# A second place for the high halves of keys and queries of three pairs, made earlier, and other float32 shares

## The chip, the cores and the metric

One core of a Trainium2 chip runs the whole program. The metric is the time of one execution on the device in microseconds (us), less is better. The core's engines are PE (TensorE: matmuls and the loading of their weights), DVE (VectorE), ACT (ScalarE), POOL (GpSimd) and SP (SyncE, which here only issues DMAs). Each engine takes its instructions in the order of its own list and waits at an instruction until what it needs is there.

## The reference

Three layers follow each other. Attention has 4 batches, 8 heads, 1152 positions and a head size of 64; neighbouring queries are averaged in twos (576 queries). A gated layer works on 2304 tokens of 512 numbers, and a soft mixture of 8 experts with 4 slots each comes last.

```python
q_pool = q.reshape(B, H, S // factor, factor, D).mean(axis=3)
scores = scale * np.matmul(q_pool, k.transpose(0, 1, 3, 2))
scores = scores - np.max(scores, axis=-1, keepdims=True)
attn = np.exp(scores)
attn = attn / (np.sum(attn, axis=-1, keepdims=True) + 1e-09)
return np.matmul(attn, v)

g = x @ w_gate
x = (g * (1.0 / (1.0 + np.exp(-g))) * (x @ w_val)) @ w_out

d = softmax of (x @ phi) over tokens;  slot_input = d.T @ x
slot_out[e] = np.maximum(slot_input[e] @ w1[e], 0.0) @ w2[e]
return (softmax of (x @ phi) over slots) @ slot_out
```

## The kernel before

Attention goes in 16 steps, one for each pair of heads; pairs and steps are counted from 0 here, so the "pairs 3, 5, 7" of the change's name are the pairs 2, 4 and 6. Every number is carried as a high and a low half in 16 bits.

**A step.** A step has 21 units. A unit's scores come from two matmuls into one bank (`unit`, L506 and L509). The second one adds the low halves and takes off the row's maximum, which lies in row D of the tile `QH`. ACT takes the exponential (L514), POOL makes the low half `PL` of the weights P (L523), and three units later the weights meet the values: three 16-bit matmuls per quarter (L550, L554, L555; L542 for the remainders), or, for a share of the units, one float32 matmul (L548), which needs no `PL`. The table `F32_PART` says how large that share is in each of the steps 0 to 7; in all others it is none.

**The maxima of the next pair.** While step i runs, `row_max` finds the row maxima of pair i + 1: 18 matmuls of 512 columns and 9 of 128 (L423) from the key's high half `kh` and from `QD`, which holds the two heads' queries on its diagonal and zeros beside it; each result is reduced by DVE (L429, L440). They share two banks (`mx`), so a matmul waits for the reduction two before it. When all are done, DVE makes `nm` (L443), ACT makes `mt` (L409) and issues the DMA (L449) that puts it into `QH`; the first L509 of step i + 1 waits for that DMA.

**The high halves.** `split_high` makes them: DVE adds the two neighbours of the queries in `qr` (L277), ACT casts `kh` and `qh` (L234), and DVE copies `qh` to `QD` in two pieces (L296). There is one tile each for `kh`, `qh` and `QD`, and the copies to `QD` are ordered behind the previous pair's `nm`. `split_pair` then makes the low halves `ql` (DVE, L325) and `kl` (POOL, L327) and moves everything to the places where the scores want it, by DMAs on SP's queue (L331 to L340).

**Other work.** From step 2 to step 8 the weights of the gated layer are prepared (L712 to L776), in step with the units; they go to six places `wgv`, the place `wgv[4]` in step 6. The gated layer itself (L811 to L816) takes part from step 4, again in step with the units, and runs on after attention; the experts come at the end. A scheduler puts the instructions in order for each engine when the program is built; `after` adds an order that it keeps.

The lines that the change and the steps below speak of:

```python
after(ins, (nm_name or nm_first)[-1])            # L297: QD behind the last nm
if steps[k - 1] in has_max and steps[k] in raw and steps[k] not in highs:   # L1168
    split_high(*steps[k])
```

Of the kernel before, what the change touches and what calls it, by code (L numbers as in the profile page):

```python
# [10 lines left out]
F16 = mybir.dt.float16  # L11
# [41 lines left out]
MOE_PACE = [(4, 0.0), (8, 1.0), (16, 5.8)]  # L53
PREP_BEG, PREP_END = 2, 8
FETCH_LEAD, FETCH_BEG = 2, 0.3
F32_PART = [0.17, 0.0, 0.17, 0.25, 0.33, 0.33, 0.34, 0.34]
F32_LAST = [99, 99, 99, 99, 99, 99, 11, 11]
VR_W = (2, 5)
VRB = 2
HNB = 1  # L60
SUBS = ["al", "l"]
# [23 lines left out]
def tile_pool_attention_glu_softmoe(  # L85
# [115 lines left out]
    nc.gpsimd.memset(KLs[1][D:D + 1, :, :], 16.0)  # L201

    QD = at.tile([P, 2, SQ], F16, name="QD")
    nc.gpsimd.memset(QD[:D, 1, :], 0.0)
    nc.gpsimd.memset(QD[D:, 0, :], 0.0)
    KHs = {}

    def load_pair(b, p):

# [61 lines left out]
    def split_high(b, p, first=None):  # L271

        kr, qr, _ = raw[b, p]

        r = slice(D if first else 0, P)
        qp = qr[r, 0, :]
        add = sub("a", b, p).tensor_tensor(out=qp, in0=qp, in1=qr[r, 1, :], op=ALU.add)  # L277

        if first:
            after(q_first[0], add.ins.name)  # L280
        if (b, p) == steps[1]:
            after(add, last_max[0])
        elif (b, p) == steps[2]:
            after(add, nm_name[-1])
        elif not first:
            not_before(add, ADD_LEAD)
        kh = at.tile([P, S], F16, tag="kh", bufs=1, name=f"kh{b}_{p}")
        KHs[b, p] = kh
        k_cast = cast("k", b, p, kh[r], kr[r])
        if mt_name:  # L290
            after(k_cast, mt_name[-1])
        qh = at.tile([P, SQ], F16, tag="qh", bufs=1, name=f"qh{b}_{p}")
        q_cast = cast("q", b, p, qh[r], qp).ins.name
        rows = [slice(0, D), slice(D, P)]
        for hd in range(0 if first else 2):
            ins = nc.vector.tensor_copy(out=QD[rows[hd], hd, :], in_=qh[rows[hd], :])  # L296
            after(ins, (nm_name or nm_first)[-1])  # L297
        highs[b, p] = r, qp, kh, qh, q_cast
        if first:
            highs_first.extend((kh, qh))  # L300
# [108 lines left out]
        return nc.scalar.activation(dst, src, AF.Copy, scale=-1.0 / 16.0, bias=math.log(PSC))  # L409

    NGQ = SQ // D
    mt_name, nm_name = [], []
    has_max = {steps[0]}

    def row_max(b, p):

        kh = KHs.pop((b, p))
        mp = at.tile([P, NGQ, 3], F32, tag="mp", bufs=2, name=f"mp{b}_{p}")
        R = S - 2 * QT

        def scores(t, g, k0, kw):
            q = QD.rearrange("p h q -> p (h q)")[:, g::NGQ]
            nc.tensor.matmul(t, q, kh[:, k0:k0 + kw], start=True, stop=True)  # L423

        for g in range(NGQ):
            for c in range(2):
                t = ps("mx", [P, QT], bufs=MXB, name=f"mx{b}_{p}_{g}_{c}")
                scores(t, g, c * QT, QT)
                ins = nc.vector.reduce_max(out=mp[:, g, c:c + 1], in_=t, axis=AX.X)  # L429
                if (b, p) == steps[1]:  # L430
                    mp_first.append(ins.ins.name)
                yield
            if g % 4 == 3 or g == NGQ - 1:

                g0 = g // 4 * 4
                n = g + 1 - g0
                t = ps("mx", [P, 4, R], bufs=MXB, name=f"mx{b}_{p}_{g}_r")
                for x in range(n):
                    scores(t[:, x, :], g0 + x, 2 * QT, R)
                nc.vector.reduce_max(out=mp[:, g0:g + 1, 2:3], in_=t[:, :n, :], axis=AX.X)  # L440
                yield
# [708 lines left out]
    for i, (b, p) in enumerate(steps):  # L1150
        for u, _ in enumerate(attn(b, p)):
# [13 lines left out]
                maxima(11 + int((MX0 - 11) * min(1.0, f / MX0_END)) + int(MXP * min(1.0, max(0.0, f - MX1_BEG) / (MX1_END - MX1_BEG))))  # L1165
            for k in (i + 1, i + 2):
                if 2 <= k < len(steps):
                    if steps[k - 1] in has_max and steps[k] in raw and steps[k] not in highs:  # L1168
                        split_high(*steps[k])
                    if steps[k] in highs or steps[k] in QHs:  # L1170
                        part = (i + f - (k - 1) - MX_BEG) / (MX_END - MX_BEG)
# [310 lines left out]
```

## Time and profile before

| what | value |
|---|---|
| median of 3 runs | 807.19 us |
| lowest and highest | 804.07 and 810.06 us |
| the profiled execution | 806.76 us |
| its span | 805.0 us |
| PE busy | 768.6 us (95%) |
| DVE, POOL and ACT busy | 521.2, 418.1 and 398.3 us |

The span is the time from the first to the last instruction; 1.8 us lie around it. A matmul's duration in the profile holds its way through the array, so a busy PE may still be able to take more: what one costs in a row of them is read from the distance between starts. An engine's idle time counts only where another one waits for it.

### The profile page before, as it was taken

How to read it: one execution, taken by the hardware profiler on the slowest of the kernel's cores; microseconds unless marked ns; L12 is line 12 of the kernel's file. 1: busy time of each engine (PE TensorE's matmuls, PEld its weight loads, DVE VectorE, ACT ScalarE, POOL GpSimd, SP SyncE). 2: the span in 40 equal slices, each digit the busy share in tenths (PEclk: the TensorE clock that was granted, in tenths of full speed). 3: DMA queues.
4: the chain of work that ended last, by engine and by line, in shares of the span. 5: the costliest groups of instructions: out<-in, count | busy, mean ns of one | idle time of the engine just before them, and what ended most of it. 6: DMA issues, size and time to landing. Idle time of an engine off the chain costs nothing.

```text
span 805.0 us, 23021 instructions
## 1 busy us (share of the span) xinstructions
PE 768.6 (95%) x9618; PEld 587.1 (73%) x9618; DVE 521.2 (65%) x1048; ACT 398.3 (49%) x770; POOL 418.1 (52%) x393
## 2 busy tenths in 40 slices
PE   6969889999999999999999999999999999999896
PEld 1546567687878777877787878777788988887544
DVE  6677889778687877676758675766552455455323
ACT  4545878777687844443544544444444222122112
POOL 9868876656567765755666666656555100000200
PEclk9989999999999999999999999999999999999799
DMA  8526878959777672533455455415112499269798
GB/s 246 140 78 194 224 199 252 236 178 210 201 230 190 200 155 61 130 94 89 116 146 138 100 117 143 90 28 107 28 27 42 99 318 279 54 184 224 255 419 359
DMA packets 115656, 132.42 MB, mean 165 GB/s; under 512 B 82272, under 2 KB 88352, under 8 KB 111328
## 3 DMA queue, kind: packets, MB, share of 16 engines
q1 hardware_dynamic: 113392, 130.92, 59.3%
q8 instruction: 75, 1.23, 0.6%
q10 hardware_dynamic: 2160, 0.04, 0.1%
q14 instruction: 29, 0.24, 0.1%
HBM read 84.10 MB, written 7.86 MB: 114 GB/s over the span
## 4 chain that ended last, share of the span: by engine, by line
PE 82%; DVE 8%; DMA 3%; ACT 2%; issue 2%; SPq 1%; POOL 0%; ACTq 0%; DVEq 0%; POOLq 0%
PE st L509 7%; PE st L506 7%; PE mx L423 6%; PE g L811 6%; PE g L816 6%; PE v L811 6%; PE v L815 6%; PE g L815 6%; PE v L816 6%; PE pv L554 3%; PE pv L550 3%; PE pv L555 3%; PE pv L542 3%; PE pv L548 3%; DVE mp L429 2%
## 5 line engine op out<-in xcount | busy, mean ns | idle before, releaser
L523 POOL TENSOR_TENSOR PL<-P 128x512 f16<-128x512 f32 (+1 forms) x303 | 314.2, 1049 | 184.9 <-ACT P L514 176.9
L514 ACT ACTIVATE P<-st 128x512 f32<-128x512 f32 (+1 forms) x336 | 192.7, 582 | 179.9 <-PE st L509 140.1
L429 DVE TENSOR_REDUCE mp<-mx 128x1 f32<-128x512 f32 x270 | 180.8, 684 | 57.9 <-PE mx L423 56.1
L509 PE MATMUL st<-QH,KL 65*128 65x512 f16 (+1 forms) x576 | 146.4, 293 | 9.9 <-DMA QH<-mt 9.7
L506 PE MATMUL st<-QQ,KK 128*128 128x512 f16 (+1 forms) x576 | 145.4, 290 | 0.7 <-ACT P L514 0.5
L550 PE MATMUL pv<-VV,P 128*128 128x65 f16 x1036 | 132.9, 194 | 0.3 <-DVE x L587 0.3
L554 PE MATMUL pv<-VV,P 128*128 128x64 f16 x1036 | 133.1, 196 | 0.0
L555 PE MATMUL pv<-VV,PL 128*128 128x65 f16 x1036 | 130.7, 193 | 0.0
L811 PE MATMUL g<-xT,wgv 128*128 128x256 f16 x432 | 117.6, 272 | 0.6 <-ACT wgv L775 0.3
L816 PE MATMUL g<-xT,wgv 128*128 128x256 f16 x432 | 117.7, 272 | 0.2 <-DVE wgv L776 0.2
L816 PE MATMUL v<-xT,wgv 128*128 128x256 f16 x432 | 117.6, 272 | 0.0
L815 PE MATMUL v<-xT,wgv 128*128 128x256 f16 x432 | 117.6, 272 | 0.0
L811 PE MATMUL v<-xT,wgv 128*128 128x256 f16 x432 | 117.6, 272 | 0.0
L815 PE MATMUL g<-xT,wgv 128*128 128x256 f16 x432 | 117.6, 272 | 0.0
L550 PEld LDWEIGHTS <-P 128*128 128x128 bf16 x1036 | 100.0, 99 | 16.6 <-issue 3.3
L423 PE MATMUL mx<-kh,QD 128*128 128x512 f16 x270 | 103.4, 394 | 3.7 <-DVE mp L429 2.1
L555 PEld LDWEIGHTS <-PL 128*128 128x128 f16 x1036 | 99.1, 100 | 9.3 <-issue 1.0
L554 PEld LDWEIGHTS <-P 128*128 128x128 bf16 x1036 | 99.1, 99 | 7.7 <-issue 0.9
L815 PEld LDWEIGHTS <-wgv 128*128 128x128 f16 x864 | 84.3, 98 | 16.0 <-issue 1.3
L816 PEld LDWEIGHTS <-wgv 128*128 128x128 f16 x864 | 84.3, 98 | 15.4 <-issue 0.4
L811 PEld LDWEIGHTS <-wgv 128*128 128x128 f16 x864 | 84.6, 98 | 14.6 <-issue 0.6
L509 PEld LDWEIGHTS <-KL 65*128 65x128 f16 x576 | 52.8, 99 | 31.6 <-issue 11.7
(209 smaller groups left out, 1237.3 us busy)
## 6 DMA issues: line engine op xcount, KB each, us to landing
w<-in_w SPq DMA_DIRECT2D x30, 1024.0 KB, 8.2
KK<-kh SPq DMA_DIRECT2D x62, 144.0 KB, 2.7
vr<-in_vP SPq DMA_DIRECT2D x14, 585.0 KB, 5.0
kr<-in_kT SPq DMA_DIRECT2D x14, 576.0 KB, 4.6
qr<-in_qT SPq DMA_DIRECT2D x14, 576.0 KB, 4.4
r<-in_w_out SPq DMA_DIRECT2D x12, 512.0 KB, 4.9
r<-in_w_gate SPq DMA_DIRECT2D x24, 256.0 KB, 4.5
r<-in_w_val SPq DMA_DIRECT2D x24, 256.0 KB, 4.9
```

The lines of the kernel that those rows point to most:

```text
L423: nc.tensor.matmul(t, q, kh[:, k0:k0 + kw], start=True, stop=True)
L429: ins = nc.vector.reduce_max(out=mp[:, g, c:c + 1], in_=t, axis=AX.X)
L506: mm = nc.tensor.matmul(t[:, o:o + w], KK[:, k], QQ[:, q0:q0 + w], start=True, stop=False)
L509: nc.tensor.matmul(t[:, o:o + w], KL[:, k], QH[:, q0:q0 + w], start=False, stop=True)
L514: ins = nc.scalar.activation(P32[:, :o], t[:, :o], AF.Exp, scale=1.0 / 16.0)
L523: nc.gpsimd.tensor_tensor(out=PL[:, :o], in0=P32[:, :o], in1=PH[:, :o], op=ALU.subtract)
L550: mm = nc.tensor.matmul(dst[:, :D + 1], PH[:, q], VV[:, c, 0, :], start=first, stop=False, skip_group_check=True)
L554: nc.tensor.matmul(dst[:, :D], PH[:, q], VV[:, c, 1, :D], start=False, stop=False, skip_group_check=True)
L555: nc.tensor.matmul(dst[:, :D + 1], PL[:, q], VV[:, c, 0, :], start=False, stop=(c == NCH - 1), skip_group_check=True)
L811: mm = nc.tensor.matmul(o, w[:, 0, d, f], xh, start=(d == 0), stop=False)
L815: nc.tensor.matmul(o, w[:, 0, d, f], xl, start=False, stop=False)
L816: nc.tensor.matmul(o, w[:, 1, d, f], xh, start=False, stop=(d == ND - 1))
```

## The change

A second `QD` and a second `kh` lie in the weight place `wgv[4]`, which holds nothing between the load of the very first pair and step 6. Pairs 2, 4 and 6 use them, all others use the old ones. For the pairs 2 to 7 the high half is made once the 13th maximum (of 18 of 512 columns) of the pair before is taken; the order behind `nm` falls away for them. POOL writes the zeros of the second `QD` at the start, two instructions. The float32 shares of the steps are set anew: larger in steps 0 to 2, smaller in 4 to 7.

```diff
--- before.py
+++ after.py
@@ -53,9 +53,11 @@
 MOE_PACE = [(4, 0.0), (8, 1.0), (16, 5.8)]
 PREP_BEG, PREP_END = 2, 8
 FETCH_LEAD, FETCH_BEG = 2, 0.3
-F32_PART = [0.17, 0.0, 0.17, 0.25, 0.33, 0.33, 0.34, 0.34]
+F32_PART = [0.33, 0.33, 0.25, 0.25, 0.17, 0.17, 0.17, 0.17]
 F32_LAST = [99, 99, 99, 99, 99, 99, 11, 11]
 VR_W = (2, 5)
+KQ_W = (2, 4, 6)
+HIGH_MX, HIGH_MP = 14, 12
 VRB = 2
 HNB = 1
 SUBS = ["al", "l"]
@@ -201,9 +203,16 @@
     nc.gpsimd.memset(KLs[1][D:D + 1, :, :], 16.0)
 
     QD = at.tile([P, 2, SQ], F16, name="QD")
-    nc.gpsimd.memset(QD[:D, 1, :], 0.0)
-    nc.gpsimd.memset(QD[D:, 0, :], 0.0)
+    kqw = wgv[-2].rearrange("p a h d n -> p (a h d n)")
+    QDs = [QD, kqw[:, 2 * S:2 * S + 2 * SQ].rearrange("p (h q) -> p h q", h=2)]
+    for t in QDs:
+        nc.gpsimd.memset(t[:D, 1, :], 0.0)
+        nc.gpsimd.memset(t[D:, 0, :], 0.0)
     KHs = {}
+
+    def in_w(b, p):
+
+        return b * NP + p in KQ_W
 
     def load_pair(b, p):
 
@@ -280,21 +289,27 @@
             after(q_first[0], add.ins.name)
         if (b, p) == steps[1]:
             after(add, last_max[0])
-        elif (b, p) == steps[2]:
-            after(add, nm_name[-1])
+        elif early_high(b * NP + p):
+            after(add, mp_names[HIGH_MP])
         elif not first:
             not_before(add, ADD_LEAD)
-        kh = at.tile([P, S], F16, tag="kh", bufs=1, name=f"kh{b}_{p}")
+        if in_w(b, p):
+            kh = kqw[:, :S]
+        else:
+            kh = at.tile([P, S], F16, tag="kh", bufs=1, name=f"kh{b}_{p}")
         KHs[b, p] = kh
         k_cast = cast("k", b, p, kh[r], kr[r])
-        if mt_name:
+        if early_high(b * NP + p):
+            after(k_cast, mp_names[HIGH_MP])
+        elif mt_name:
             after(k_cast, mt_name[-1])
         qh = at.tile([P, SQ], F16, tag="qh", bufs=1, name=f"qh{b}_{p}")
         q_cast = cast("q", b, p, qh[r], qp).ins.name
         rows = [slice(0, D), slice(D, P)]
         for hd in range(0 if first else 2):
-            ins = nc.vector.tensor_copy(out=QD[rows[hd], hd, :], in_=qh[rows[hd], :])
-            after(ins, (nm_name or nm_first)[-1])
+            ins = nc.vector.tensor_copy(out=QDs[in_w(b, p)][rows[hd], hd, :], in_=qh[rows[hd], :])
+            if not early_high(b * NP + p):
+                after(ins, (nm_name or nm_first)[-1])
         highs[b, p] = r, qp, kh, qh, q_cast
         if first:
             highs_first.extend((kh, qh))
@@ -409,17 +424,23 @@
         return nc.scalar.activation(dst, src, AF.Copy, scale=-1.0 / 16.0, bias=math.log(PSC))
 
     NGQ = SQ // D
-    mt_name, nm_name = [], []
+    mt_name, nm_name, mp_names = [], [], []
+
+    def early_high(i):
+
+        return i > 1 and (i in KQ_W or i - 1 in KQ_W)
     has_max = {steps[0]}
 
     def row_max(b, p):
 
         kh = KHs.pop((b, p))
+        qdiag = QDs[in_w(b, p)]
+        mp_names.clear()
         mp = at.tile([P, NGQ, 3], F32, tag="mp", bufs=2, name=f"mp{b}_{p}")
         R = S - 2 * QT
 
         def scores(t, g, k0, kw):
-            q = QD.rearrange("p h q -> p (h q)")[:, g::NGQ]
+            q = qdiag.rearrange("p h q -> p (h q)")[:, g::NGQ]
             nc.tensor.matmul(t, q, kh[:, k0:k0 + kw], start=True, stop=True)
 
         for g in range(NGQ):
@@ -427,6 +448,7 @@
                 t = ps("mx", [P, QT], bufs=MXB, name=f"mx{b}_{p}_{g}_{c}")
                 scores(t, g, c * QT, QT)
                 ins = nc.vector.reduce_max(out=mp[:, g, c:c + 1], in_=t, axis=AX.X)
+                mp_names.append(ins.ins.name)
                 if (b, p) == steps[1]:
                     mp_first.append(ins.ins.name)
                 yield
@@ -1165,7 +1187,11 @@
                 maxima(11 + int((MX0 - 11) * min(1.0, f / MX0_END)) + int(MXP * min(1.0, max(0.0, f - MX1_BEG) / (MX1_END - MX1_BEG))))
             for k in (i + 1, i + 2):
                 if 2 <= k < len(steps):
-                    if steps[k - 1] in has_max and steps[k] in raw and steps[k] not in highs:
+                    if early_high(k):
+                        seen = n_rm[0] >= MX0 + MXP * (k - 2) + HIGH_MX
+                    else:
+                        seen = steps[k - 1] in has_max
+                    if seen and steps[k] in raw and steps[k] not in highs:
                         split_high(*steps[k])
                     if steps[k] in highs or steps[k] in QHs:
                         part = (i + f - (k - 1) - MX_BEG) / (MX_END - MX_BEG)
```

The instruction lists show what moves. In the names the last number is a running one, the first ones are pair (within its batch), head or unit; line numbers of the change are higher than before (L423 is L444, L429 is L450, L440 is L462, L443 is L465, L277 is L286, L296 is L310, L325 is L340, L509 is L531). First DVE at the end of step 0, before:

```order
L587 TENSOR_TENSOR x_0_1_836<-pv_0_1_543,rs_0_1_835 128x384
L429 TENSOR_REDUCE mp_1_347<-mx_1_8_1_601 128x1
L440 TENSOR_REDUCE mp_1_347<-mx_1_8_r 128x1
L443 TENSOR_REDUCE nm_1_626<-mp_1_347 128x9
L277 TENSOR_TENSOR qr_2_492<-qr_2_492 128x576
L296 COPY QD<-qh_2_651 64x576 x2
L325 TENSOR_TENSOR ql_2_757<-qr_2_492,qh_2_651 128x576
L429 TENSOR_REDUCE mp_2_775<-mx_2_0_0_776 128x1
```

And with the change, from the 13th maximum of pair 1 on:

```order
L450 TENSOR_REDUCE mp_1_347<-mx_1_6_0_519 128x1
L286 TENSOR_TENSOR qr_2_484<-qr_2_484 128x576
L450 TENSOR_REDUCE mp_1_347<-mx_1_6_1_528 128x1
L310 COPY wgv_84<-qh_2_524 64x576 x2
L340 TENSOR_TENSOR ql_2_734<-qr_2_484,qh_2_524 128x576
L450 TENSOR_REDUCE mp_1_347<-mx_1_7_0_531 128x1
L450 TENSOR_REDUCE mp_1_347<-mx_1_7_1_534 128x1
```

and some rows later, up to `nm` of pair 1:

```order
L450 TENSOR_REDUCE mp_1_347<-mx_1_8_1_546 128x1
L609 TENSOR_TENSOR x_0_1_807<-pv_0_1_562,rs_0_1_806 128x384
L462 TENSOR_REDUCE mp_1_347<-mx_1_8_r 128x1
L450 TENSOR_REDUCE mp_2_752<-mx_2_0_0_753 128x1
L465 TENSOR_REDUCE nm_1_552<-mp_1_347 128x9
```

The sum, the two copies and the low half of pair 2's queries (`qr_2`, the copy from `qh_2`, `ql_2`) stood behind pair 1's `nm`; now they stand among pair 1's maxima, and one maximum of pair 2 stands ahead of that `nm`.

PE at the same place, before, where pair 1's last maxima are followed by the scores `st_1_0` of step 1:

```order
L423 MATMUL mx_1_8_0_591<-kh_1_292,QD 128x512
L423 LDWEIGHTS QD
L423 MATMUL mx_1_8_1_601<-kh_1_292,QD 128x512
L423 LDWEIGHTS QD
L423 MATMUL mx_1_8_r<-kh_1_292,QD 128x128
L509 LDWEIGHTS KL_102
L509 MATMUL st_1_0_746<-QH_1_464,KL_102 128x512
L509 LDWEIGHTS KL_102
L509 MATMUL st_1_1_797<-QH_1_464,KL_102 128x512
L506 LDWEIGHTS KK_1_462
L506 MATMUL st_1_2_819<-QQ_1_463,KK_1_462 128x512
```

With the change, from the second maximum of pair 2 on:

```order
L444 LDWEIGHTS wgv_84
L444 MATMUL mx_2_0_1_756<-wgv_84 128x512
L444 LDWEIGHTS wgv_84
L444 MATMUL mx_2_1_0_759<-wgv_84 128x512
L444 LDWEIGHTS wgv_84
L444 MATMUL mx_2_1_1_765<-wgv_84 128x512
L444 LDWEIGHTS wgv_84
L444 MATMUL mx_2_2_0_775<-wgv_84 128x512
L444 LDWEIGHTS wgv_84
L444 MATMUL mx_2_2_1_787<-wgv_84 128x512
L531 LDWEIGHTS KL_102
L531 MATMUL st_1_0_725<-QH_1_454,KL_102 128x512
```

Six maxima of pair 2 (`mx_2_0_0` to `mx_2_2_1`, now from `wgv`) stand ahead of the matmul that waits for pair 1's maximum. At the end of step 1 there are three maxima of pair 3 ahead of step 2's first scores, and the last maximum of pair 2 stands ahead of twelve units' values.

SP's queue at the start of step 1, before:

```order
L339 DMA KL_101<-kl_2_759 64x1152
L340 DMA QH_2_756<-qh_2_651 64x576
L632 DMA_TRANSPOSE xT_895<-xhl_0_511 128x4x128
L632 DMA_TRANSPOSE xT_897<-xhl_0_511 128x4x128
L217 DMA kr_3_940<-in_kT 128x1152
L220 DMA qr_3_941<-in_qT 128x1152
L701 DMA r_1161<-in_w_out 128x1024
```

With the change:

```order
L354 DMA KL_101<-kl_2_736 64x1152
L355 DMA QH_2_733<-qh_2_524 64x576
L226 DMA kr_3_899<-in_kT 128x1152
L229 DMA qr_3_900<-in_qT 128x1152
L237 DMA vr_3_903<-in_vP 128x1170
L654 DMA_TRANSPOSE xT_856<-xhl_0_503 128x4x128
L654 DMA_TRANSPOSE xT_858<-xhl_0_503 128x4x128
L226 DMA kr_0_1425<-in_kT 128x1152
```

The load of pair 3's keys and queries (`kr_3`, `qr_3`) stood behind two transposes that wait for DVE; now it stands ahead of them. The load of the pair after it (`kr_0` of the next batch) has moved ahead of the first weights.

## Rows read from the trace of the kernel before

**Rows 1.** The page, part 1: busy time, share of the span, instructions.

```profile
PE 768.6 (95%) x9618; PEld 587.1 (73%) x9618; DVE 521.2 (65%) x1048; ACT 398.3 (49%) x770; POOL 418.1 (52%) x393
```

**Rows 2.** Steps 1, 2, 3, 4 to 7: length, busy time; then PEclk, DMA share, GB/s.

```profile
54.90:85.00 30.10, 25.78 (x328) 16.37 (x328) 23.00 (x34) 15.75 (x30) 25.20 (x24) 0.85 0.63 176
85.00:115.50 30.50, 27.18 (x362) 19.66 (x362) 27.04 (x50) 25.17 (x50) 23.82 (x21) 1.00 0.78 220
115.50:144.20 28.70, 27.14 (x355) 20.55 (x355) 22.89 (x46) 24.62 (x50) 19.80 (x18) 1.00 0.86 239
144.20:278.90 134.70, 134.13 (x1667) 105.25 (x1667) 108.36 (x205) 104.09 (x206) 86.67 (x79) 1.00 0.80 210
```

**Rows 3.** Waits of PE: total us, times, longest.

```profile
PE st L509 <- DMA QH<-mt: 9.7, 4, 4.4
```

**Rows 4.** Chain of waits, 60 to 160 us: start, us, what.

```profile
67.15 5.41 DMA qr<-in_qT
...
82.17 2.80 DMA QH<-mt
...
110.69 4.74 DMA QH<-mt
...
140.60 3.56 DMA QH<-mt
```

**Rows 5.** In order of time, 46 to 60 us: start, us, what [idle before].

```profile
46.96 1.43 DVE L429 TENSOR_REDUCE mp<-mx 128x1 f32<-128x512 f32 x2 [1.01 <-PE mx L423]
...
51.52 0.18 DVE L443 TENSOR_REDUCE nm<-mp 128x9 f32<-128x27 f32 x1
...
54.30 2.36 POOL L327 TENSOR_TENSOR kl<-kr,kh 128x1152 f16<-128x1152 f32 x1 [2.11 <-ACT kh L234]
...
54.83 3.06 DVE L296 COPY QD<-qh 64x576 f16<-64x576 f16 x2 [2.03 <-ACT qh L234]
54.89 1.01 PE L509 MATMUL st<-QH,KL 65*128 65x512 f16 x2 [4.39 <-DMA QH<-mt]
...
57.92 1.48 DVE L325 TENSOR_TENSOR ql<-qr,qh 128x576 f16<-128x576 f32 x1
```

**Rows 6.** Busy time in stretches of 4 us; columns as in Rows 2.

```profile
56.00:60.00 4.00, 3.17 (x9) 1.19 (x9) 3.96 (x5) 1.28 (x4) 4.00 (x4) 0.50 0.56 132
60.00:64.00 4.00, 4.00 (x33) 2.42 (x32) 2.89 (x5) 2.15 (x5) 2.99 (x5) 0.53 0.57 127
```

**Rows 7.** Busy time in a stretch of step 2; columns as in Rows 2.

```profile
85.90:110.90 25.00, 23.89 (x320) 17.29 (x319) 24.43 (x47) 22.55 (x47) 19.73 (x19) 1.00 0.76 218
```

**Rows 8.** Chain of waits: matmuls in a row on PE.

```profile
45.45 0.92 PE pv L548 x8
...
85.61 0.43 PE mx L423 x2
```

**Rows 9.** PE in order of time, 43.5 to 47.5 us.

```profile
43.97 0.19 PE L550 MATMUL pv<-VV,P 128*128 128x65 f16 x1
...
44.06 0.19 PE L550 MATMUL pv<-VV,P 128*128 128x65 f16 x1
```

**Rows 10.** Groups of instructions by form: busy us, mean ns, idle before.

```profile
L523 POOL TENSOR_TENSOR PL<-P 128x512 f16<-128x512 f32 x259 | 278.0, 1084 | 163.7 <-ACT P L514 156.7 <-DMA KL<-kl 4.5 <-DVE mp L429 1.2
...
L296 DVE COPY QD<-qh 64x576 f16<-64x576 f16 x30 | 18.6, 622 | 2.2 <-ACT qh L234 2.0
...
L325 DVE TENSOR_TENSOR ql<-qr,qh 128x576 f16<-128x576 f32 x14 | 13.0, 931 | 0.0
...
L277 DVE TENSOR_TENSOR qr<-qr 128x576 f32<-128x576 f32 x14 | 12.6, 903 | 0.8 <-DMA qr<-in_qT 0.5 <-issue 0.3
```

**Rows 11.** POOL in order of time, the first 30 us.

```profile
3.15 0.58 POOL L204 MEMSET QD<- 64x576 f16 x1
```

**Rows 12.** DVE in order of time, 85 to 146 us.

```profile
109.73 1.13 DVE L296 COPY QD<-qh 64x576 f16<-64x576 f16 x2
```

**Rows 13.** POOL in order of time, 104 to 114 us.

```profile
108.56 1.82 POOL L523 TENSOR_TENSOR PL<-P 128x512 f16<-128x512 f32 x2 [0.29 <-ACT P L514]
```

## The prediction, made before the change was run

> **What bounds the kernel now.** I read the busy shares first: PE is busy 95% of the span, DVE 65% [rows 1]. So only time in which PE stands, its clock, or PE's own work can matter much. Next the stretches by step [rows 2]: from step 4 on PE has no idle time to give back (134.13 busy of 134.70 us); the loss lies in steps 1 to 3, with 30.10 − 25.78 = 4.32 us, 3.32 us and 1.56 us, and step 1 has a mean granted clock of 0.85. The waits name the place [rows 3]: the matmul that takes off the maximum waits for the DMA that brings it, 9.7 us in four waits, the longest 4.4. The chain of waits shows three of these DMAs, each ending where a step begins: 84.97, 115.43 and 144.16 us [rows 4]. The fourth, at the end of step 0, ends at 54.9 [rows 5]. Pair 1's `nm` is there at 51.52, PE waits 4.39 us for its way into `QH`, and meanwhile no maximum of pair 2 can be taken, because `QD` is copied at 54.83 and takes 3.06 us for two copies beside POOL's `kl`. Behind this idle time the granted clock is 0.50 and 0.53 between 56 and 64 us [rows 6]: the lower level, 1.2 GHz. Step 2 is DVE's: 24.43 busy of 25.00 us before its last maximum [rows 7].
>
> The sum is made against the profiled execution, 806.76 us (span 805.0 and 1.76 around it), which is 0.43 under the median of the runs shown. A difference of 1%, 8.1 us, is about what a measurement of this kernel can tell from none.
>
> **Prices.** A matmul of 512 columns for the maxima takes 0.43 / 2 = 0.215 us in a row. A float32 unit of values is four matmuls of 0.92 / 8 = 0.115 us, 0.46 us [rows 8]; in 16 bits it is twelve, and three of them take 44.06 − 43.97 = 0.09 us, so 0.36 [rows 9]. A float32 unit thus costs PE 0.10 us more and saves POOL one `PL`, 1.084 us [rows 10].
>
> **Start.** Two more zero fills of 0.58 us stand in POOL's list [rows 11]; they delay what follows by up to 1.2 us. Two small copies have moved behind the queries' low half, and PE waits at the start for DMAs and DVE too. Lower bound 0, upper 1.2; I take +0.3, nearer to nothing.
>
> **End of step 0 and step 1.** On DVE the sum, two copies, `ql` of pair 2 and one maximum of it stand ahead of pair 1's `nm` now. Uncontended means [rows 10] and a maximum of 1.43 / 2 [rows 5] give 0.90 + 2 × 0.62 + 0.93 + 0.7 = 3.8 us; DVE idles 1.01 us there [rows 5], so `nm` comes 2.8 us later. With the contended durations of rows 5 (3.06 for the copies, 1.48) it is 0.90 + 3.06 + 1.48 + 0.7 − 1.0 = 5.1. I take 3.0, since the copies' mean over 30 is near the uncontended row. Step 1 then starts at 57.9 instead of 54.9, but six maxima of pair 2 fill the wait. Casts on ACT and `kl` on POOL (2.36 us [rows 5]) also move ahead of the last exponentials and `PL`; values follow three units later, which covers that. If the cover is gone, it is part of the 5.1.
>
> Length of step 1: of its 25.78 busy us, 7.17 lie in the two stretches at half clock [rows 6], so about 3.6 are the clock's. 25.78 − 3.6 = 22.2; seven float32 units add 0.7; six maxima are already done (−1.3), three of pair 3 come in (+0.65): 22.25 at full clock, 25.85 if the clock falls as long as before. I take 24.5: the middle, and 0.4 for waits that are left. The load of pair 3's queries, which lands at 72.56 [rows 4], stands ahead of two transposes on SP now, so it comes earlier; the transposes wait for DVE's work for the gated layer, which starts at step 4, so a few us later cost them nothing (if they were late, step 4 would show PE waiting for `xT`). Step 2 starts at 57.9 + 24.5 = 82.4, not 85.0: **−2.6**; bounds 57.7 + 22.25 = 79.95 (−5.05) and 60.0 + 25.85 = 85.85 (+0.85).
>
> **Step 2.** Three of pair 3's maxima are taken earlier, and at the end other PE work stands behind the last maximum, so the 4.74 us of the DMA [rows 4] no longer stand bare. The floor is set twice: PE's busy 27.18 and 0.2 for two more float32 units, and DVE's busy 27.04 [rows 2]. Both full at once is not to be had: I take 27.8 of 30.5, **−2.7**; bounds −3.1 and 0 (DVE still full, then late with the next maximum).
>
> **Step 3.** Idle time of 1.56 us, all at the last boundary, with 6 us of other PE work to cover it by the number of instructions that now stand there. The float32 share stays. **−1.3**, bounds −1.56 and 0.
>
> **Steps 4 to 7.** Counted in the lists, float32 units go from 5, 7, 7, 3 and 4 (steps 3 to 7) to 5, 3, 4, 2 and 2: ten fewer in steps 4 to 7, on a PE that is always busy: 10 × 0.10 = **−1.0**. POOL gets ten `PL` more, 10.8 us on 86.67 of 134.70 us [rows 2]; its idle time covers them. Step 0's three more units (0.3 us) lie where PE waits at the end. Steps 8 to 15 keep their order.
>
> Sum: 0.3 − 2.6 − 2.7 − 1.3 − 1.0 = −7.3, so 806.76 − 7.3 = **799.5 us**.
>
> **Rivals.**
> 1. *The clock falls again.* Six matmuls of 0.215 us, one for each reduction of 0.7, leave PE idle most of that wait, and that is how it stood when the clock fell before. If `nm` also comes 5.1 us later, step 1 gives +0.85 instead of −2.6: 806.76 − 3.85 = 802.9. For it: DVE is the limit there, and its group got longer; against it: scores of step 1 follow sooner behind each maximum.
> 2. *POOL and DVE hold each other up.* The copies took 3.06 us beside POOL's `kl` [rows 5] and 1.13 us at 109.73 [rows 12]. In the change they stand in the midst of POOL's stream of `PL`. If each group pays 1.93 for the copies and 1.48 − 0.93 for `ql`, that is 2.5 us: 2.1 at the end of step 0 and 2.5 in step 2, where DVE is full; steps 1 and 3 hide it. −7.3 + 4.6 = −2.7: 804.1. Against it: at 109.73 the copies ran beside two `PL` of 0.91 us each [rows 13], and neither was stretched; and the mean of 30 copies is 0.62 [rows 10]. The Trainium skill ("SBUF — State Buffer", Who interferes with whom) says that a DVE copy in a two-port mode, or a DVE operation with two SBUF inputs, and a GpSimd operation that reads SBUF shut each other out for a whole instruction, while reductions never contend. By that rule this rival would be the forecast; rows 5 agree with it, rows 13 don't.
> 3. *Everything fits.* Clock kept, step 1 at its PE work, steps 2 and 3 at theirs: 0 − 5.05 − 3.1 − 1.56 − 1.0 = −10.7: 796.1.
> 4. *Slower.* DVE's group (sum, copies, `ql`) stands between two maxima that come by turns in two banks. PE takes its instructions in order: when the bank of the second to last maximum isn't reduced, scores and values wait behind the maximum. In steps 4 to 7 a maximum comes each 134.70 / 4 / 18 = 1.9 us [rows 2], and one free bank covers that much. Uncontended the group is 3.1 us long, contended 0.90 + 3.06 + 1.48 = 5.4; beyond 1.9 us PE loses the rest, 3.5 at most. In steps 4 and 5, where PE has nothing to spare, that is 7.0; with the gains of steps 2 and 3 (4.0) eaten as well and rival 2's 4.6 in part (2.1), −7.3 + 7.0 + 4.0 + 2.1 = +5.8, and with other DVE work inside the groups 3 us more: 812.6 to 815.6. For it: before, this group stood behind `nm`, where no maximum could be waiting. Against it: matmuls for maxima have given PE few waits so far, and in the change's list value matmuls stand between them.
>
> That the change doesn't do what it says is excluded: the lists show the second place in use.
>
> **Numbers.** Forecast 0.53 (796 to 804; somewhat more than half of it under 799.1, the bound for faster by 1%), rival 1 0.16, rival 2 0.10, rival 3 0.12, rival 4 0.09. Faster 0.28 + 0.12 = 0.40; within 1% 0.25 + 0.16 + 0.10 = 0.51; slower 0.09. The range: 796.1 less 2.7, by which the fastest run shown lies under the profiled execution, gives 793.4, so 793; above, the upper bounds together give 1.2 + 0.85 − 1.0 = +1.05, 807.8, which needs all at once, so 807. It leaves out rival 4 and the far tails, some 0.15.
>
> **What would show it.** Right: in step 1's first 10 us a granted clock near 1.00 or at least shorter at 0.5, step 2 starting near 82.4, PE's wait for `QH` far below 9.7 us, copies near 0.6 us, steps 4 to 7 about 1 us shorter. Wrong: a new wait of PE's maxima matmuls for DVE in steps 1 to 5 (rival 4), copies of over 1 us beside `PL` (rival 2), a clock of 0.5 after 58 us (rival 1).

## The result and the profile after

The change made the kernel slower: 818.08 us (median of 4 runs, 813.32 to 821.36) against 806.86 for the kernel before in the same runs, a ratio of 1.0108 with a 95% interval of 1.0069 to 1.0146. The profiled execution has a span of 816.4 us, 11.4 more than before.

The page's first part, and then the same stretches as before (steps 1, 2, 3, and 4 to 7; columns as in [rows 2]), with three waits of PE (total us, times, longest):

```profile
PE 776.1 (95%) x9611; PEld 590.7 (72%) x9611; DVE 525.7 (64%) x1048; ACT 398.0 (49%) x770; POOL 419.7 (51%) x393
```

```profile
61.20:89.70 28.50, 27.01 (x296) 19.55 (x296) 15.96 (x28) 15.25 (x30) 17.47 (x16) 0.89 0.40 132
89.70:122.10 32.40, 29.36 (x356) 21.66 (x354) 26.17 (x48) 24.98 (x50) 20.80 (x19) 0.95 0.77 218
122.10:150.90 28.80, 27.21 (x351) 19.98 (x352) 24.95 (x49) 24.91 (x50) 21.07 (x19) 1.00 0.90 243
150.90:295.60 144.70, 138.51 (x1768) 106.60 (x1767) 112.44 (x207) 106.81 (x210) 101.65 (x91) 0.99 0.77 198
```

```profile
PE mx_r L444 <- DVE mp L450: 5.6, 5, 2.0
PE st L531 <- DMA QH<-mt: 3.9, 2, 2.4
PE g L833 <- DMA xT<-xhl: 1.5, 1, 1.5
```

Against [rows 1, 2, 3]: PE is busy 7.5 us longer, though its wait for the DMA of the maximum fell from 9.7 to 3.9 us. A wait for the maxima's bank has come instead, and one in step 4 for the transposes `xT` that feed the gated layer. The last stretch of [rows 2] ends some 6 us before step 8 begins; the kernel before has up to there

```profile
144.20:284.50 140.30, 139.27 (x1721) 109.61 (x1721) 110.01 (x208) 106.80 (x210) 90.88 (x82) 1.00 0.79 206
```

so in steps 4 to 7 PE stood for 1.0 us and now stands for 6.2 (144.70 − 138.51). Where each step begins, by its first matmul that takes off a maximum:

| step | 1 | 2 | 3 | 4 | 5 | 6 | 7 | 8 |
|---|---|---|---|---|---|---|---|---|
| before, us | 54.9 | 85.0 | 115.5 | 144.2 | 180.1 | 215.0 | 247.6 | 284.5 |
| after, us | 61.2 | 89.7 | 122.1 | 150.9 | 187.1 | 225.0 | 259.2 | 295.6 |
| after less before | 6.3 | 4.7 | 6.6 | 6.7 | 7.0 | 10.0 | 11.6 | 11.1 |

So step 0 loses 6.3, step 1 gives 1.6 back, step 2 loses 2, steps 5 and 6 lose 4.6. Three places show how.

**The end of step 0.** The change in order of time (start, us, engine):

```profile
46.48 2.38 POOL L342 TENSOR_TENSOR kl<-kr,wgv 128x1152 f16<-128x1152 f32 x1 [0.21 <-ACT wgv L243]
46.84 2.64 DVE L286 TENSOR_TENSOR qr<-qr 128x576 f32<-128x576 f32 x1
50.21 0.62 DVE L310 COPY wgv<-qh 64x576 f16<-64x576 f16 x2
50.87 0.76 DVE L340 TENSOR_TENSOR ql<-qr,qh 128x576 f16<-128x576 f32 x1
56.04 0.17 DVE L465 TENSOR_REDUCE nm<-mp 128x9 f32<-128x27 f32 x1
56.49 0.53 ACTq L471 DMA_DIRECT2D QH<-mt  x1
56.62 0.45 SPq L229 DMA_DIRECT2D qr<-in_qT  x1
57.17 0.59 SPq L237 DMA_DIRECT2D vr<-in_vP  x1
61.20 1.01 PE L531 MATMUL st<-QH,KL 65*128 65x512 f16 x2 [2.39 <-DMA QH<-mt]
```

DVE's sum of the queries (`qr`) ends when POOL's `kl` has ended and its own work is then done: 2.64 us for what takes 0.75 alone. `nm` comes at 56.04, 4.5 us later than in [rows 5]. Then pair 3's queries and values (and its keys, from 55.99) are loaded just when the small DMA of the maximum is under way. In the chain of waits it takes

```profile
56.49 4.67 DMA QH<-mt
```

where it took 2.87 before (issued at 51.98, PE goes on at 54.85). 4.5 + 1.8 is the 6.3 that step 0 lost. Not all of the 4.5 is the moved group's: with the new shares alone (e1 below) `nm` comes at 52.82, 1.3 us later than before.

**The clock.** The granted clock in three stretches at the end of step 0 and behind it, and three in step 5 (columns as in [rows 2]):

```profile
54.00:56.00 2.00, 1.38 (x3) 0.41 (x3) 1.99 (x6) 0.32 (x1) 1.60 (x1) 0.50 0.71 156
58.00:62.00 4.00, 1.51 (x4) 0.37 (x3) 1.54 (x3) 0.17 (x1) 0.00 (x0) 0.50 1.00 352
62.00:66.00 4.00, 4.00 (x15) 2.70 (x14) 1.29 (x2) 1.51 (x3) 2.08 (x2) 0.50 0.15 62
208.00:210.00 2.00, 0.60 (x6) 0.24 (x3) 1.97 (x3) 1.18 (x2) 2.00 (x3) 1.00 0.36 84
210.00:212.00 2.00, 1.35 (x8) 0.74 (x8) 2.00 (x5) 0.08 (x1) 0.90 (x1) 0.75 1.00 337
212.00:214.00 2.00, 2.00 (x12) 1.39 (x10) 1.76 (x5) 1.17 (x3) 1.04 (x1) 0.50 1.04 394
```

The clock had fallen by 54 us, before the six maxima of pair 2 (54.80 to 58.81), and they did not bring it back. Summed over stretches of 2 us between 50 and 300 us, PE stood at the lower level (1.2 GHz) for 20.4 us, 10.2 before. A PE that is busy all the time loses half of such a time, so this is up to 5.1 of the 11.4 us. The 20.4 are 13.6 from 54 us on, 3.4 in step 2 and 3.4 in step 5. e1 below has 20.5 us of it as well, in a span of 809.7 us, so the clock alone does not make the loss.

**Step 5.** PE, DVE and POOL in order of time, where the clock falls again:

```profile
204.87 2.39 POOL L342 TENSOR_TENSOR kl<-kr,kh 128x1152 f16<-128x1152 f32 x1 [0.74 <-ACT kh L243]
...
206.44 2.04 DVE L310 COPY QD<-qh 64x576 f16<-64x576 f16 x2 [0.40 <-ACT qh L243]
206.89 0.41 PE L444 MATMUL mx<-wgv 128*128 128x512 f16 x1
207.21 3.69 POOL L545 TENSOR_TENSOR PL<-P 128x512 f16<-128x512 f32 x3
208.52 1.48 DVE L340 TENSOR_TENSOR ql<-qr,qh 128x576 f16<-128x576 f32 x1
209.92 0.68 DVE L450 TENSOR_REDUCE mp<-mx 128x1 f32<-128x512 f32 x1
210.65 0.40 PE L444 MATMUL mx_r<-wgv 128*128 128x128 f16 x4 [2.05 <-DVE mp L450]
```

The first copy waits out `kl`, the second one the first `PL`, `ql` the next: 3.5 us for what takes 1.4 alone, and POOL's three `PL` take 1.11, 1.10 and 1.52 us instead of 1.04. The maximum whose matmul ended at 207.3 is reduced at 209.92, so the bank comes free late and PE, whose next instruction needs it, stands for 2.05 us; then the clock falls. In step 2 it is the same group (copies 1.60, `ql` 1.48 beside three `PL` of 1.23), and what comes late is the normalisation for which PE's values wait, 1.7 us. All in all the group did not grow much: between 40 and 290 us the sums, copies and `ql` of eight pairs take DVE 29.5 us, 26.7 before, where they collided too ([rows 5]). New is where it stands: among maxima that PE waits for, and no longer behind `nm`.

### The profile page after: what moved, and what is told of

Read it like the earlier page. It is cut to its first block, busy times and chain, and to the rows that moved or that the text cites. A ratio compares the mean times of both kernels' runs of the same rounds, so it can differ in the third digit from the quotient of the medians.

```text
span 816.4 us, 23007 instructions
## 1 busy us (share of the span) xinstructions
PE 776.1 (95%) x9611; PEld 590.7 (72%) x9611; DVE 525.7 (64%) x1048; ACT 398.0 (49%) x770; POOL 419.7 (51%) x393
## 3 DMA queue, kind: packets, MB, share of 16 engines
q8 instruction: 75, 1.23, 0.6%
## 4 chain that ended last, share of the span: by engine, by line
PE 81%; DVE 6%; DMA 4%; ACT 3%; POOL 3%; issue 2%; SPq 1%; DVEq 0%; ACTq 0%; POOLq 0%
PE st L531 7%; PE st L528 7%; PE mx L444 6%; PE v L833 6%; PE v L837 6%; PE v L838 6%; PE g L833 6%; PE g L837 6%; PE g L838 6%; PE pv L576 4%; PE pv L572 3%; PE pv L577 3%; PE pv L564 3%; PE pv L570 2%; DVE mp L450 2%
## 5 line engine op out<-in xcount | busy, mean ns | idle before, releaser
L450 DVE TENSOR_REDUCE mp<-mx 128x1 f32<-128x512 f32 x270 | 180.1, 683 | 61.6 <-PE mx L444 59.2
L531 PE MATMUL st<-QH,KL 65*128 65x512 f16 (+1 forms) x576 | 147.7, 293 | 4.2 <-DMA QH<-mt 3.9
L444 PE MATMUL mx<-kh,QD 128*128 128x512 f16 x216 | 82.5, 393 | 1.6 <-DVE mp L450 1.4
L531 PEld LDWEIGHTS <-KL 65*128 65x128 f16 x576 | 53.3, 99 | 30.7 <-issue 12.4
```

The source lines that it names most:

```text
L531: nc.tensor.matmul(t[:, o:o + w], KL[:, k], QH[:, q0:q0 + w], start=False, stop=True)
```

## The experiments

Theory: POOL and DVE hold each other up where both read from SBUF; the stops of PE that follow from it lower the clock; and loads slow the small DMA. Rivals: the new shares; the length of DVE's group by itself; POOL's `PL`, which stand behind `kl` now.

**Which half of the change.** e1, the kernel before with the shares:

```diff
-F32_PART = [0.17, 0.0, 0.17, 0.25, 0.33, 0.33, 0.34, 0.34]
+F32_PART = [0.33, 0.33, 0.25, 0.25, 0.17, 0.17, 0.17, 0.17]
```

> The kernel before with the new float32 shares alone (no second place, high halves as before). Theory (the loss comes from where the high halves are made): twelve float32 units more in steps 0 to 2 cost PE at most 1.2 us, ten fewer in steps 4 to 7 give 1.0 back, so 805 to 809 us, no difference to before. Rival (the shares did it): most of the 11 us, so 814 or more, with the loss in steps 0 to 2.

809.11 us, ratio to before 1.0021 (0.9985 to 1.0057): no difference in the whole. Inside, the time moves: `nm` at the end of step 0 comes 1.3 us later, and step 1 takes 32.7 us instead of 30.1:

```profile
52.82 0.18 DVE L443 TENSOR_REDUCE nm<-mp 128x9 f32<-128x27 f32 x1
```

```profile
56.30:89.00 32.70, 29.56 (x317) 21.19 (x318) 21.07 (x37) 16.49 (x31) 18.55 (x17) 0.88 0.57 162
```

e2, the changed kernel with the old shares:

> The changed kernel with the old float32 shares. Theory: the loss stays, 815 to 821 us, with pair 1's maximum about 4 us later than before and PE's waits for the maxima's bank in steps 2 and 5. Rival (the shares did it): near 807 us.

825.70 us, 1.0213 (1.0166 to 1.0260). The places carry the loss, and more than all of it: with them the new shares help by some 7 us, alone they don't. In e2 PE's waits for the maxima's bank are 9.5 and 8.4 us, the copies to the two places between 40 and 290 us take 18.1 us for 14 of them (12.7 for 16 in the change), and PE is at the lower clock for 41 us.

**POOL's low half of the keys.** e3 holds it until DVE's `ql` is made:

```diff
+        if early_high(b * NP + p):
+            held(k_low, q_low)
```

(`held` makes the first instruction wait for the second one's result; the lines that define it are left out here.)

> The changed kernel in which POOL makes the low half of the keys of pairs 2 to 7 only when DVE has made that of the queries, so that POOL's 2.4 us no longer lie beside DVE's sum and copies. Theory (DVE and POOL shut each other out): the sum at the end of step 0 falls from 2.64 to about 0.8 us, the copies in step 5 from 2.04 to about 0.7, the end of step 0 comes about 2 us sooner, and the short stop and half clock in step 5 go: 811 to 815 us. Rival (the group is too long for the two banks even alone, or only POOL's PL count): no change, 817 to 819. Second rival (POOL's low half is now late for the scores): PE waits for KL and the time is over 820.

810.67 us, 1.0017 (0.9995 to 1.0039), 7 us better than the change. DVE and POOL at the end of step 0:

```profile
46.75 0.75 DVE L290 TENSOR_TENSOR qr<-qr 128x576 f32<-128x576 f32 x1
48.24 0.62 DVE L314 COPY wgv<-qh 64x576 f16<-64x576 f16 x2
...
49.73 2.38 POOL L346 TENSOR_TENSOR kl<-kr,wgv 128x1152 f16<-128x1152 f32 x1 [1.55 <-DMA KK<-wgv]
53.47 0.18 DVE L471 TENSOR_REDUCE nm<-mp 128x9 f32<-128x27 f32 x1
57.51 1.01 PE L537 MATMUL st<-QH,KL 65*128 65x512 f16 x2 [1.10 <-DMA QH<-mt]
```

The sum is down to 0.75, `nm` 2.6 and step 1 3.7 us sooner. But `kl` now also stands behind `PL` that it stood ahead of, so the third rival was open. e13 is e3 with work in that old place that reads nothing:

```diff
+        if early_high(b * NP + p):
+            for _ in range(2):
+                fill = nc.gpsimd.memset(kl[r], 0.0)
+                after(fill, k_cast_name[b, p])
```

> The kernel of e3 with two useless fills of the tile of the keys' low half (about 1.2 us each) on POOL, where the changed kernel has the low half itself: as long, ahead of the same PL, but they read nothing. If POOL and DVE shut each other out over what they read from SBUF (theory), DVE's sum stays near 0.8 us beside the fills, the end of step 0 stays that of e3 (step 1 from 57 to 58.5), and the whole is 810 to 814. Rival (e3 won because POOL's PL no longer stand behind 2.4 us of other work): back to the change, 816 to 820, with values or exponentials waiting for POOL and the sum still short. Third outcome (any work on POOL holds DVE up): the sum is 2 us or more beside the fills.

818.51 us, 1.0109 (1.0066 to 1.0151), by its total the rival; by step 0 the theory:

```profile
46.25 2.18 POOL L349 MEMSET kl<- 128x1152 f16 x2
46.88 0.75 DVE L290 TENSOR_TENSOR qr<-qr 128x576 f32<-128x576 f32 x1
48.36 1.16 DVE L315 COPY wgv<-qh 64x576 f16<-64x576 f16 x2
```

The sum takes 0.75 us wholly beside the fills, and step 1 starts at 57.6. This is what the Trainium skill ("SBUF — State Buffer", Who interferes with whom) says: a DVE operation with two SBUF inputs contends with a GpSimd operation that reads SBUF, not with one that only writes it. The later steps lost it again (step 2 took 37.7 us; at its end the DMA of the maximum took 8.88 us, and PE waited 4.7 us; in e3 it took 7.25, and PE waited 3.6). POOL has 2.2 us more work per pair here, so this told nothing of them, and the third rival stays open. The next three leave POOL's work as long as in the change. e9 moves the copies to ACT:

```diff
-            ins = nc.vector.tensor_copy(out=QDs[in_w(b, p)][rows[hd], hd, :], in_=qh[rows[hd], :])
+            cp = nc.scalar.copy if early_high(b * NP + p) else nc.vector.tensor_copy
+            ins = cp(QDs[in_w(b, p)][rows[hd], hd, :], qh[rows[hd], :])
```

> The changed kernel with the copies into the two places on ACT, and POOL's low half of the keys where the change has it. Theory: the copies' 1.2 to 2.1 us per pair leave DVE, the wait of 2.0 us behind them in step 5 shrinks, but the sum at the end of step 0 still stands 2.6 us beside POOL's low half, so step 1 starts near 59 to 60: 810 to 815, between the change and e7. Rival (copies are all of it): like e7, 805 to 808. Rival (the keys' low half is all of it): 816 or more.

817.28 us, 1.0100 (1.0062 to 1.0138): nothing gained, a little outside what the theory gave. The sum still takes 2.64 us beside `kl`. e15 keeps the copies on DVE and has fills instead of `kl`; e16 has both edits:

```diff
-        k_low = nc.gpsimd.tensor_tensor(out=kl[r], in0=kr[r], in1=kh[r], op=ALU.subtract)
+        if early_high(b * NP + p):
+            for _ in range(2):
+                k_low = nc.gpsimd.memset(kl[r], 0.0)
+                after(k_low, k_cast_name[b, p])
+        else:
+            k_low = nc.gpsimd.tensor_tensor(out=kl[r], in0=kr[r], in1=kh[r], op=ALU.subtract)
```

> The changed kernel where POOL, for pairs 2 to 7, fills the tile of the keys' low half with zeros (two fills, 2.2 us) instead of computing it: the keys' low half is left out of these pairs' scores. POOL works as long in the same place ahead of the same PL, but reads nothing. Theory (POOL's reading beside DVE's two inputs costs): the sum at the end of step 0 is 0.75 instead of 2.64 us, step 1 starts at 57 to 59 instead of 61.2, and the whole is 809 to 814. Rival (the PL that stand behind it): as the change, 816 to 820.

> The kernel of e9 (copies on ACT, low half of the keys in the change's place, 817.3) with the same two fills for the keys' low half of pairs 2 to 7, which is left out. Nothing on POOL but PL reads beside DVE's group now. Theory: like e7 within 4 us, 804 to 811. Rival (the PL behind POOL's work): like e9, 815 to 819, with the sum and ql short all the same.

e15: 818.20 us, 1.0115 (1.0074 to 1.0155); e16: 811.67, 1.0037 (1.0004 to 1.0070). Between e9 and e16 only POOL's `kl` differs, 2.4 us that read against 2.2 that don't. DVE's sums and low halves between 40 and 290 us fall from 22.0 to 15.6 us (the sum at the end of step 0 from 2.64 to 0.75), and by the medians 5.6 us of the total go with it, though the two intervals just overlap: the reading costs. e16 is still 5 us over e7 below, where nothing stands ahead of those `PL`, so the third rival may hold a part as large as that; this is not settled further. By its total e15 came out as the rival said. Its step 1 starts at 58.2 as expected, 3 us sooner than in the change, but step 2 only at 92.1. DVE, POOL and PE in step 1 of e15, and then its stretches:

```profile
74.09 4.68 POOL L551 TENSOR_TENSOR PL<-P 128x512 f16<-128x512 f32 x4
...
74.53 1.83 DVE L311 COPY QD<-qh 64x576 f16<-64x576 f16 x2
...
76.40 1.48 DVE L341 TENSOR_TENSOR ql<-qr,qh 128x576 f16<-128x576 f32 x1
78.53 0.58 PE L450 MATMUL mx<-wgv 128*128 128x512 f16 x1 [1.78 <-DVE mp L456]
```

```profile
76.00:78.00 2.00, 0.59 (x2) 0.23 (x2) 1.97 (x3) 0.60 (x2) 2.00 (x3) 1.00 1.01 381
78.00:80.00 2.00, 1.47 (x5) 0.82 (x5) 2.00 (x5) 0.93 (x2) 0.78 (x1) 0.63 0.83 254
80.00:82.00 2.00, 2.00 (x20) 2.00 (x20) 0.34 (x2) 0.33 (x1) 0.00 (x0) 0.50 0.91 303
...
86.00:88.00 2.00, 2.00 (x33) 1.90 (x32) 0.00 (x0) 1.01 (x2) 0.93 (x1) 0.50 0.00 0
```

Without `kl` the group meets the `PL` instead, PE stands 1.78 us, and runs at 1.2 GHz from 78.5 to 88.8 us. So in e9 and e15 the two collisions don't add up: with either one left PE still stands behind DVE's reductions, up to 1.6 us at a time in e9 and 1.78 in e15, and both have 20.5 us at the lower level, like the change. e3 does not fit this: its later copies still meet `PL`, and it is 7 us faster than e15. Why is not settled.

**The loads.** e5 holds pair 3's loads behind the DMA of the maximum, every list otherwise the same:

```diff
-        nc.sync.dma_start(out=vr, in_=vP[b, p])
+        v_load = nc.sync.dma_start(out=vr, in_=vP[b, p])
+        if (b, p) == steps[3]:
+            for ins in (k_load, q_load, v_load):
+                held(ins, mt_name[0])
```

> The changed kernel with its own order on every engine, but pair 3's three loads on SP wait until the DMA that brings pair 1's maximum has landed. Theory (three loads of 1.7 MB beside that DMA make it 4.67 us instead of 2.9): it takes about 2.9, step 1 starts 1.8 us sooner, and since pair 3's queries are wanted only some 12 us later, the whole is 1.5 to 2.5 us shorter: 815 to 817. Rival (the DMA is slow whatever lies beside it): over 4 us still, 818. Rival (SP's queue is held up and something behind it comes late): 818 or more with a new wait for a DMA.

816.57 us, 1.0101 (1.0076 to 1.0127). The chain of waits of e5:

```profile
56.53 2.86 DMA QH<-mt
```

2.86 instead of 4.67, step 1 at 59.4 instead of 61.2, as expected; the total cannot be told from the change's by the two ratios. e4 meant the same by issuing the loads from ACT (shown for the keys; queries and values likewise use `e`):

```diff
-        k_load = nc.sync.dma_start(out=kr[r], in_=kT[b, p, r])
+        e = nc.scalar if (b, p) == steps[3] else nc.sync
+        k_load = e.dma_start(out=kr[r], in_=kT[b, p, r])
+        if (b, p) == steps[3]:
+            after(k_load, mt_name[0])
```

> The changed kernel with the load of pair 3 (keys, queries, values, 1.7 MB) issued by ACT right behind the DMA that brings pair 1's maximum, instead of by SP ahead of it. Theory (the loads share the DMA engines with it): that DMA falls from 4.67 to about 2.9 us, step 1 starts 1.8 us sooner, and 1.5 to 2.5 us of it reach the end: about 816. Rival (DVE is the limit in step 1 anyway, or the loads come late for pair 3's maxima): 818 or more, with a new wait for the queries' load. Rival (the two small halves are slow whatever lies beside): the DMA still takes over 4 us.

823.97 us, 1.0175 (1.0134 to 1.0216). Two of the three loads came ahead of the small DMA in ACT's list, which was issued only at 58.61, when the queries had landed (58.54), and then took 2.87. So the edit did not do what it meant to: it shows what a place behind loads in ACT's list costs, and says nothing of the theory.

**The place.** e6 makes the high halves behind the 18th maximum, e8 uses the second place for pairs 4 and 6 alone, on top of e3, e10 has one place but the copies on ACT and the new shares:

```diff
-HIGH_MX, HIGH_MP = 14, 12
+HIGH_MX, HIGH_MP = 21, 17
```

> The changed kernel with the high halves made behind the 18th instead of the 13th maximum: the second place stays, the group of DVE stands at the end of the maxima, and POOL's low half of the keys moves with it. If it is the place among the maxima that costs (PE's matmul waits for its bank behind the group), PE's waits for the bank in steps 2 and 5 vanish and it is 807 to 812. If it is DVE and POOL shutting each other out that costs, wherever they stand, copies of 1 to 2 us stay and it is 814 or more.

```diff
-KQ_W = (2, 4, 6)
+KQ_W = (4, 6)
```

> The kernel of e3 with the second place used for pairs 4 and 6 only, so that pairs 2 and 3 are made as before. Theory: steps 0 and 1 are those of the kernel with the float32 shares alone (step 1 starts near 56.3, step 2 near 89), the later steps those of e3; 808 to 812. If the second place gives something in step 1 (e3's step 2 starts at 86.1), this is slower than e3 by up to 3 us.

```diff
-            ins = nc.vector.tensor_copy(out=QD[rows[hd], hd, :], in_=qh[rows[hd], :])
+            cp = nc.scalar.copy if 2 <= b * NP + p < 8 else nc.vector.tensor_copy
+            ins = cp(QD[rows[hd], hd, :], qh[rows[hd], :])
```

> The kernel before with the new shares and the copies of pairs 2 to 7 on ACT, but with one place only, so behind pair 1's maximum. If e7's gain comes from taking the copies from DVE, this is near e7, 804 to 807. If it needs the second place, which lets pair 2's maxima fill the wait, this stays at 806 to 810 with PE's wait for the DMA of the maximum at 8 to 10 us in four.

e6: 822.23 us, 1.0166 (1.0137 to 1.0195): the group collides there too (a sum of 2.60 us at 82.12 beside `kl` at 81.73), and the next maxima wait for the copies up to 5.1 us. This other place is no better, so the place among the maxima is not the whole cause. e8: 819.68, 1.0124 (1.0097 to 1.0151), 8 us over what was expected. Its steps 1 and 2 start at 56.8 and 88.0, near e1's as expected, but step 2 takes 36.7 us and the waits for the DMA of the maximum are 11.4 in four; why is not settled. e10: 814.85, 1.0070 (1.0039 to 1.0102), slower than before, with 8.6 us of that wait left. The copies on ACT give nothing by themselves.

**Versions that win.** e7 is e3 with e9's copies on ACT, e11 is e7 with e5's hold, e14 has that hold for the loads of pairs 3 to 8, and e12 is e7 with the old shares. The diff is that of e14 against e11.

> The kernel of e3 (POOL's low half of the keys behind DVE's of the queries) with the copies into the two places on ACT. Theory: copies that meet a PL on POOL still took 1.05 instead of 0.3 us in e3; without them DVE's group is 0.6 to 2.2 us shorter per pair and PE's waits for the maxima's bank (6.4 us in e3) shrink: 805 to 809. Rival (ACT is now late with its exponentials, 25 of 31 us busy in steps 2 and 3): 811 or more, with more waits of PE for P.

> The kernel of e7 with pair 3's loads held until pair 1's maximum has landed, as in e5. That DMA takes 3.3 us in e7, and 2.9 undisturbed, so 0.4 us at most: 0 to 1 us under e7. Rival (the hold makes pair 3's queries late): slower than e7.

```diff
-        if (b, p) == steps[3]:
+        if 3 <= b * NP + p <= 8:
             for ins in (k_load, q_load, v_load):
-                held(ins, mt_name[0])
+                held(ins, mt_name[b * NP + p - 3])
```

> The kernel of e7 with the loads of pairs 3 to 8 held until the maximum of the pair two before has landed, not only pair 3's as in e11 (804.7). In e7 and e11 the DMA of the maximum at the end of step 2 still took 5 us beside such a load. Theory: 2 us less there, PE's last waits for it go: 801 to 805, and faster than the kernel before by 0.5 to 1%. Rival (later loads make a later pair's sum late): no better than e11.

> The kernel of e7 with the old float32 shares. With the old shares the changed kernel was 7 us slower (e2), by copies of 1.05 us and more beside POOL's PL and POOL's low half. Theory (the shares matter only because fewer PL leave DVE alone): with the copies on ACT and the low half held, most of that goes, so 804 to 810. Rival (POOL's count of PL is a limit of its own in steps 1 to 4): 812 or more, with PE waiting for values.

e7: 806.66 us, 0.9965 (0.9945 to 0.9986); e11: 804.72, 0.9935 (0.9900 to 0.9970). Both beat both kernels, the kernel before by 0.35 and 0.65%. e11 by steps 1, 2, 3 and 4 to 7:

```profile
56.10:83.60 27.50, 26.76 (x287) 19.05 (x287) 14.99 (x27) 16.63 (x32) 16.62 (x16) 0.88 0.57 176
83.60:114.60 31.00, 28.38 (x359) 21.10 (x358) 27.09 (x50) 26.22 (x52) 20.75 (x19) 1.00 0.83 233
114.60:141.80 27.20, 26.20 (x336) 19.17 (x337) 22.57 (x43) 25.82 (x52) 20.34 (x18) 1.00 0.91 238
141.80:277.50 135.70, 131.75 (x1729) 101.91 (x1728) 106.89 (x202) 109.14 (x214) 97.32 (x88) 1.00 0.79 210
```

The clock is at 1.00 from step 2 on, 10.2 us at the lower level as before. The last stretch can't be held against the 140.30 us before as it stands: 249 matmuls of the gated layer (`g` and `v`) lie in it, 288 before and in the change, and 39 at some 0.11 us, their distance in a row, are 4 us of work that comes later. e14: 822.04, 1.0171 (1.0135 to 1.0207). SP takes its list in order, and its waits show what a hold at its head costs (SP's own waits and PE's, total, times, longest):

```profile
SPq L230 <- DMA QH<-mt: 31.9, 4, 13.3
```

```profile
PE g L843 <- DMA xT<-xhl: 4.8, 1, 4.8
```

The transposes behind it come late. e12: 810.37, 0.9995 (0.9973 to 1.0016). By the medians the new shares are still worth 3.7 us without the collisions (the intervals overlap), where they were worth 7.6 with them; what the 3.7 come from is open.

## Why the prediction failed

- **What bounds the kernel**: right. The waits named fell from 9.7 to 3.9 us. That they were worth their length was wrong: what took their place costs the same.
- **Start**: the first scores were not later (14.9 us, 15.0 before).
- **Prices**: that of a float32 unit is wrong. [rows 8] has eight records in 0.92 us, and I took four of them for a unit. Step 1 of the change has 18 whole units (and three made of remainders). Twelve in 16 bits leave 48 records of each of their three matmuls, so the six in float32 are eight records each:

```profile
L570 PE MATMUL pv<-vr,P 128*128 128x65 f32 x48 | 7.1, 297 | 0.2 <-DVE x L609 0.2
...
L572 PE MATMUL pv<-VV,P 128*128 128x65 f16 x48 | 6.6, 196 | 0.0
```

  A unit thus takes 0.92 us and not 0.46, 0.56 more than in 16 bits and not 0.10. By the counts of records there are ten whole units more in steps 0 to 2 and nine fewer in steps 4 to 7, so in the whole the error nearly cancels. That e1 came out even is luck as far as this price goes.
- **End of step 0**: `nm` came 4.5 us later, inside 2.8 to 5.1, but not by the copies (0.62). The sum, which I priced at its mean of 0.90, is most of it: e3, without its collision, has `nm` 2.6 us sooner. Another 1.3 are the shares' (e1), which I put at 0.3 us that PE's wait would hide. That `kl` moves with the group was counted as covered work of POOL; that it would stand beside the group was not asked.
- **The load on SP's queue**, counted as a gain and its displaced transposes as free: its collision with the DMA of the maximum, 1.8 us, was not in the sum. This and the former put step 1 at 61.2, past the bound of 60.0. Step 4 does show PE waiting for `xT`, 1.5 us, the sign that I had named for late transposes; e7 and e11 have 1.7 us of it too, and which order makes them late was not tried.
- **Length of step 1**: 28.5 instead of 24.5, past the bound of 25.85. It is not the clock: by the mean clocks 0.89 and 0.85, step 1 has 6.3 us at the lower level, and 9.0 before. The price of float32 is enough for it: six whole units are 3.4 us, where I had 0.7 for seven, and 2.7 is what lies between 25.85 and 28.5. e1's step 1, longer by 2.6, shows the same.
- **Step 2**, −2.7 forecast, is +2: the late normalisation, the clock behind it (3.4 us at the lower level), and two more float32 units at 1.1 instead of 0.2. **Step 3**, −1.3, is 0.
- **Steps 4 to 7**, −1.0 forecast, are +4.4. At the right price the shares should have given 5.0, so some 9.4 us were lost. PE stands 5.2 us more: its waits are 2.9 us behind DVE's reductions, 1.5 for the DMA of the maximum at the start of step 7 and 1.5 for the transposes. The lower clock in step 5 is up to 1.7. The rest, some 2.5 us, is open.
- **The step that failed is the dismissal of rival 2**, and with it of rival 4: the group was priced uncontended and, in steps 4 to 7, its wait put at nothing. I read [rows 12, 13] as copies beside two `PL` without stretch. In single instructions the first of these `PL` (1.04 us) had ended at 109.60, before the copies began, and the second, of 384 columns, ran its 0.83 us to 110.38. The first copy waited it out, 0.81 us to 110.54; the other one takes 0.3:

```profile
109.73 0.81 DVE L296 COPY QD<-qh 64x576 f16<-64x576 f16 x1
```

  So 1.13 was itself a stretched pair, and the mean of 0.62 in [rows 10] mixes kinds: 0.3 alone, up to 1.05 beside a `PL`, and 2.00 for the first copy beside `kl` in [rows 5]. In the change the sum took 2.64 us for 0.75 at the end of step 0, and copies and `ql` took 3.5 for 1.4 in step 5, where PE stood 2.05 us behind them. The rule of the Trainium skill ("SBUF — State Buffer", Who interferes with whom) was set against these rows in the prediction; read as single instructions, they agree with it.
- **Rivals**: what came is rival 4's place (PE behind the group, 2.05 us in step 5) with rival 2's cause and rival 1's clock. Priced apart, at 812.6 to 815.6, 804.1 and 802.9, none held the time; the clock, 5.1 us, stood in none but the first, and there only as a gain lost.

## What to carry to other kernels

When work is moved, ask what runs beside it on an engine that it was seen to collide with (here POOL beside DVE), not only what it stands ahead of; and look at single instructions before a mean is used as a price. Count the records of a unit before a price per record is used for it. Where an engine without slack takes its list in order, a stop of 2 us may cost it more than 2 us, as in step 5, where the clock fell behind it; and removing one of two collisions may show nothing, as in e9 and e15. A load issued early is not free: here it met the smallest and most urgent DMA of the step.

## What the runs showed of the hardware

- A copy of 64x576 in 16 bits takes 0.3 us on DVE alone and 1.05 beside `PL`; a sum of 128x576 float32 0.75 alone, 2.64 beside a subtraction on POOL (e9: the same) and 0.75 beside a fill (e13). POOL pays too: 1.10 to 1.52 instead of 1.04 us per `PL` in step 5.
- A DMA of 2.2 KB takes 2.86 us with the loads held, 4.67 beside three loads.
- After PE stood for 1.78 us in e15, with little work for some 2 us around it, it ran at 1.2 GHz from 78.5 to 88.8 us, though it was busy nearly all the time from 78.5 us on.
- A float32 matmul of the values (128x65) leaves two records of some 0.115 us each: a unit of four such matmuls takes 0.92 us, and one of twelve in 16 bits 0.36 by the same distances.
